# Linear attention and a SiLU MLP in one kernel: sums of x kept in one tile, two of them placed sooner, and two streams of pieces exchanged in the last half group

## The chip, the cores and the metric

The kernel runs on one core of a Trainium2 chip. The metric is device time in microseconds (us), the median of several runs. Engines are named as in the profile: PE is the matrix engine, PEld its weight loads, DVE the vector engine, ACT the scalar engine, POOL the GpSimd engine, SP the engine that here only issues DMAs.

## The reference

```python
# q, k, v, alpha: (4, 8, 768, 48), float32; w_in and w_out: float64
for t in range(S):
    state = alpha[:, :, t, :, None] * state + einsum('bhd,bhe->bhde', k[:, :, t], v[:, :, t])
    y[:, :, t] = einsum('bhd,bhde->bhe', q[:, :, t], state)
x = y.transpose(0, 2, 1, 3).reshape(3072, 384)
h = x @ w_in              # w_in  384 x 2048
g = h * (1 / (1 + exp(-h)))
out = g @ w_out           # w_out 2048 x 384
```

That is a decayed running state for each of 32 heads, and an MLP on what it gives; the output is 3072 rows of 384 numbers.

## The kernel before, in words

**Two halves at once.** The attention part walks over 24 blocks of 128 tokens (`NT = 24`), one block a step, four slots a step. The MLP part trails behind it: four blocks make a group of 512 tokens, six groups in all (grp 0 to 5, `GB = 4`, `NG = 6`). Its work is cut into generators that advance one piece at a time; `fill(step, slot)` runs pieces after each slot until the work done reaches what is due. Once the start is over (`late` is filled), every matmul is recorded in program order, so PE runs exactly the order in which pieces are called.

**The w_in side.** Groups 2 to 5 use a bilinear scheme with fewer products: `enter(grp, pair)` forms 20 block products (`PRODUCTS`) of sums of x and sums of w_in, for one of two halves ("pairs") of the columns. It has seven pieces; here they are E0 to E6. E0 to E5 have three products each and E6 two; one product is four PE instructions in the trace. Products go into three PSUM banks `ps_m`, are evicted by ACT (L936) or combined by DVE (L944, L587), pass SiLU on ACT (L941), and end with one addition for each half of the tokens, `side_by_side` (L1019). E6 holds the last two products; after them come, on DVE, the sums written `tt(s[0])` and `tt(s[3])`, on ACT the SiLU of each, and then the two `side_by_side`.

**The sums of x.** `sums_x(grp)` is one piece of no counted work: it takes a tile `xc` of 11 blocks of 128x256 from a pool with one buffer, and DVE forms 11 sums in a fixed order (`SUMS_X`, lines L582 to L587). The first two, blocks 9 and 6, need only the first half of a group's tokens; the third needs the second half. E0's products read sums 9, 6 and 6; E1's first product reads sum 15, which is the eighth of the list.

**The w_out side.** `leave(grp, h)` forms, for half a group, seven products with blocks of w_out; pieces L0 to L6, of eight matmuls, that is 16 PE instructions in the trace. They go to two PSUM banks `ps_o`. L6 fills the first bank and DVE adds to it into the output tile (`store`, L1042); L0 of the next `leave` fills that same bank again, from new. L0 reads first the g of pair 0, then (from its fifth matmul) that of pair 1.

**The order.** `pieces` is a list written out by hand. For group grp the list holds `sums_x(grp)`, and then by turns one piece of `leave(grp - 1, h)` and one of `enter(grp, pair)`: L0 E0 L1 E1 ... for pair 0 with h 0, and the same for pair 1 with h 1. After the last group, `leave(5, 0)` and `leave(5, 1)` follow alone. `pieces[done][2]` is the number of blocks whose x must exist; `phases` says where groups end in the list, and `marks` at which slot each is due.

**The audits.** `audit()` reads alpha, w_in and w_out once more, a piece a time, into one buffer (`late["look"]`, one buffer), and two DVE reductions a piece (L685) keep a largest and a smallest value. SP issues the next load (L677) when the second reduction of the one before has ended. The weights are 8-byte numbers, so one piece of w_out, 128x384, is 384 KB; of these there are 16. The reductions stand in DVE's order between the work of the pieces, in an order that is kept. From all of them DVE makes a flag that decides at the end whether the general path must run.

**DVE's order** is made by a scheduler except where `tc.keep_in_program_order` is called: the sums of x and the reductions keep their order among each other, all else is placed by it.

Of the kernel before, what the change touches and what calls it, by code (L numbers as in the profile page):

```python
# [8 lines left out]
F32 = mybir.dt.float32  # L9
# [10 lines left out]
def general(  # L20
# [322 lines left out]
SUMS_X = (  # L343
    (9, 1, 2, 1, 4), (6, 1, 0, 1, 2), (7, 1, 2, 1, 3), (8, 1, 0, 1, 7), (10, -1, 1, -1, 8),
    (11, 1, 5, -1, 10), (12, 1, 4, 1, 11), (15, -1, 0, 1, 12), (16, 1, 1, -1, 15),
    (13, 1, 4, 1, 7), (14, -1, 6, 1, 11),
)
# [8 lines left out]
def quotients(  # L356
# [22 lines left out]
    late = {}  # L379
# [25 lines left out]
    GB = 4  # L405
    NG = NT // GB
    HF = NFT // 2
    NQ = NFT // 4
    TB = GB * C // 2
    HO = HD // 2  # L410

    def pool(name, bufs=1, space=None):
        kw = {} if space is None else {"space": space}
        return ctx.enter_context(tc.tile_pool(name=name, bufs=bufs, **kw))
# [51 lines left out]
    def load(n, names="akq"):  # L466
        if n == NT:
            return
        c = ctxs.setdefault(n, dict(zip(("ci", "b"), divmod(n, B))))
        b, rows = c["b"], slice(c["ci"] * C, c["ci"] * C + C)  # L470
        for name, src in (("a", alpha), ("k", k), ("q", q)):
            if name not in names:
                continue
            x = src[b, :, rows, :]
            if n < NA:
                c[name] = nat[name][n % NIN]
                nc.sync.dma_start(c[name][:, :, 0:D], x.transpose([1, 0, 2]))
                continue

            c[name] = late["quads"][name]
            for u in range(2):
                for i in range(2):
                    r = 64 * u + 32 * i
                    nc.sync.dma_start(
                        c[name][r : r + 32, 32 * (1 - i) :][:, 0 : 4 * NP * D].rearrange(
                            "p (g c) -> p g c", g=NP),
                        x[u::2].rearrange("h (b j) d -> b h (j d)", j=4))
# [90 lines left out]
    def combine(to, sa, a, sb, b):  # L580
        if sa == sb == 1:
            return dve.tensor_tensor(to, a, b, ALU.add)  # L582
        if sa == 1:
            return dve.tensor_tensor(to, a, b, ALU.subtract)
        if sb == 1:
            return dve.tensor_tensor(to, b, a, ALU.subtract)  # L586
        return dve.scalar_tensor_tensor(to, a, -1.0, b, ALU.mult, ALU.subtract)  # L587
# [100 lines left out]
    xts, xcs = {}, {}  # L688
# [183 lines left out]
    def block_x(grp, at):  # L872

        if at < 2 * NKT:
            return xts[2 * grp + at % 2][:, at // 2, :]
        return xcs[grp][:, at - 2 * NKT, :]

    def sums_x(grp):
        xcs[grp] = late["xc"].tile([128, len(SUMS_X), TB], F32, name="xc")
        for to, sa, a, sb, b in SUMS_X:  # L880
            tc.keep_in_program_order(
                combine(block_x(grp, to), sa, block_x(grp, a), sb, block_x(grp, b)))
        yield
# [8 lines left out]
    turn = [0, 1, 2]  # L892
# [217 lines left out]
    def group(grp):  # L1110
        return [[(enter(grp, pair), 12, GB * grp + GB)] * 7 for pair in range(2)]

    def output(grp):
        return [[(leave(grp, h), 12, GB * grp + GB)] * 7 for h in range(2)]

    def both(x, y):
        for i in range(max(len(x), len(y))):
            pieces.extend(x[i : i + 1] + y[i : i + 1])

    pieces = []  # L1120
# [4 lines left out]
    phases = [len(pieces)]  # L1125
# [2 lines left out]
    phases.append(len(pieces))  # L1128
    before = output(1)
    for grp in range(2, NG):  # L1130
        pieces.append((sums_x(grp), 0, GB * grp + GB))
        for x, y in zip(before, group(grp)):
            both(x, y)
        phases.append(len(pieces))
        before = output(grp)
    pieces += before[0] + before[1]
# [17 lines left out]
    def settle():  # L1154

        first.close()
        late.update(look=pool("look"), part=pool("part"), xc=pool("xc"), turn=pool("turn"),
                    wx=pool("wx").tile([128, 8, NQ, 128], F32, name="wx"))
        quads = pool("quads")
        late["p"] = pool("p").tile([128, NP * W + 1], F32, name="p")  # L1160
        late["quads"] = {name: quads.tile([128, 32 + 4 * NP * D], F32, name=f"{name}t") for name in "akq"}
        for name, t in late["quads"].items():
            gps.memset(t, 1.0 if name == "a" else 0.0)
        load(NA)
# [20 lines left out]
    for step in range(STEPS):  # L1185
        if step == 1:
            load(NIN)
        stages = [[(scores, 1)], [(products, 0)], [(values, 1)], [(states, 1)]]
        if step == 1:

            stages = stages[1::-1] + stages[2:]
        elif step >= NA:
            stages = [[(land, 1), (scores, 1)], [(products, 0)], [(quotient, 0)],
                      [(values, 1), (states, 1), (flip, 0)]]
        for slot, group in enumerate(stages):
            for stage, lag in group:
                n = step - lag
                if not 0 <= n < NT:
                    continue
                stage(n)  # L1200
                if stage is values:
                    bridged = n + 1
                if stage is states and n + 1 + NIN < NA:
                    load(n + 1 + NIN)
                if stage is states and n + NV < NT:
                    load_v(n + NV)
            if step * SLOTS + slot == (NA + 1) * SLOTS - 1:
                x = decayed.rearrange("p (o i c) -> p o i c", o=2, c=C)
                for r, o in later:
                    gps.memset(x[r, o, :, 0:CH], 0.0)  # L1210
            fill(step, slot)
            if step * SLOTS + slot >= NA * SLOTS - 1 and conv_done[1] == NFT and not late:
                settle()
# [35 lines left out]
@with_exitstack  # L1249
def kernel(  # L1250
    ctx: ExitStack,
    tc: tile.TileContext,
    q: bass.AP,
    k: bass.AP,
    v: bass.AP,
    alpha: bass.AP,
    moe_w_in: bass.AP,
    moe_w_out: bass.AP,
    out: bass.AP,
):  # L1260


    flag = ctx.enter_context(tc.tile_pool(name="flag", bufs=1))
    small = flag.tile([1, 1], I32, name="small")
    args = (q, k, v, alpha, moe_w_in, moe_w_out, out)
    within = quotients(tc, small, *args)
    with tc.If(within < 1, label="general"):
        general(tc, *args)
# [30 lines left out]
```

## Time and profile before

| what | value |
|---|---|
| median of 3 runs | 559.94 us (559.90 to 559.98) |
| span of the profiled execution, first to last instruction | 558.1 us |
| what lies between that span and the median | 1.8 us |
| busy PE, PEld, DVE, ACT, POOL | 541.4, 488.8, 445.1, 208.4, 75.9 us |
| mean granted PE clock | 0.994 |
| reductions of the audits (L685) | 65, from 247.2 to 518.4 us |
| last block of attention leaves PE | about 443 us |
| pair 1 of group 5 begins on PE | about 479 us |

The page gives busy time by engine for one profiled execution. The list of waits names, for each engine, what ended its idle time. The timeline gives start, length, engine, line, operation and tiles, the number of instructions merged, and in brackets the idle time before it. A row's length is that of its instructions from the first start to the last end; neighbours on DVE and PE overlap, so the step from start to start is what an instruction costs in a full queue. Starts of PE instructions are 0.163 us apart for a 128x192 product and 0.216 us for a 128x256 one where nothing is waited for, which makes a piece L 2.61 us, E0 to E5 2.59 us and E6 1.73 us.

### The profile page before, as it was taken

To read this page: it belongs to the slowest core of one execution; us is meant where nothing else is said; L and a number is where in the kernel's file an instruction comes from. 1 tells how busy PE (TensorE), PEld (TensorE's weight loads), DVE (VectorE), ACT (ScalarE), POOL (GpSimd) and SP (SyncE) were. 2 spreads that over 40 slices of the span, in tenths; PEclk is the share of its full clock that TensorE was granted. 3 is DMA by queue.
4 is the path that set the end of the run, shared out by engine and by line. 5 is a ranking of instruction groups with operands and counts; after the bars stand their busy time and mean duration, and the time that the engine had idled before them with its cause. 6 is when DMAs were issued, how large, how long until landed. Compare 5 with 4: busy or idle time off the path is not lost. (4 is left out here: it accounts for less than half of the span.)

```text
span 558.1 us, 12640 instructions
## 1 busy us (share of the span) xinstructions
PE 541.4 (97%) x5026; PEld 488.8 (88%) x5026; DVE 445.1 (80%) x801; ACT 208.4 (37%) x466; POOL 75.9 (14%) x146
## 2 busy tenths in 40 slices
PE   5999999999999999999999999999999999999996
PEld 3788887998899898899999999988998999998996
DVE  5887889974999799997998986998894775857531
ACT  3456643223333243353353353353263341432200
POOL 4100010221211211021021021021121000001000
PEclk9799999999999999999999999999999999999999
DMA  9999861164445525355445654717712122333101
GB/s 218 255 276 177 232 189 40 38 164 108 126 131 136 142 62 134 88 145 157 129 109 142 194 141 115 198 22 179 180 48 84 53 99 95 111 109 106 38 25 32
DMA packets 99220, 70.13 MB, mean 126 GB/s; under 512 B 56272, under 2 KB 88656, under 8 KB 99152
## 3 DMA queue, kind: packets, MB, share of 16 engines
q1 hardware_dynamic: 97232, 65.30, 44.6%
q0 software_dynamic: 1920, 3.93, 2.0%
q8 instruction: 41, 0.67, 0.5%
q14 instruction: 27, 0.22, 0.1%
HBM read 61.34 MB, written 7.86 MB: 124 GB/s over the span
## 5 line engine op out<-in xcount | busy, mean ns | idle before, releaser
L388 PE MATMUL ps_o<-w_out,g 128*128 128x192 f32 x768 | 134.7, 329 | 1.1 <-DVE o L1042 0.9
L388 PEld LDWEIGHTS ps_o<-w_out,g 128*128 128x128 f32 x768 | 125.4, 190 | 5.1 <-DVE o L1042 2.3
L388 PE MATMUL ps_m<-xt,w_in 128*128 128x256 f32 x480 | 113.6, 383 | 1.5 <-ACT xt L851 1.1
L388 PEld LDWEIGHTS ps_m<-xt,w_in 128*128 128x128 f32 x480 | 89.1, 190 | 14.4 <-ACT xt L851 1.6
L388 PE MATMUL ps_o<-wt,g 128*128 128x192 f32 x576 | 99.7, 326 | 0.0
L388 PEld LDWEIGHTS ps_o<-wt,g 128*128 128x128 f32 x576 | 95.1, 190 | 1.6 <-issue 0.2
L388 PE MATMUL ps_m<-xc,w_in 128*128 128x256 f32 x288 | 70.7, 382 | 0.0
L685 DVE TENSOR_REDUCE seen<-bits 128x1 f32<-128x384 int32 (+2 forms) x65 | 42.5, 689 | 24.0 <-DMA bits<-in_moe_w_out_dram 19.6
L388 PEld LDWEIGHTS ps_m<-xc,w_in 128*128 128x128 f32 x288 | 53.6, 190 | 7.0 <-DVE g L944 0.3
L941 ACT ACTIVATE g<-g 128x1024 f32<-128x1024 f32 x32 | 33.0, 1056 | 59.0 <-DVE g L944 59.0
L1033 DVE TENSOR_TENSOR g<-g 128x512 f32<-128x512 f32 x72 | 49.8, 708 | 6.1 <-PE ps_o L388 6.1
L1045 POOL DMA_DIRECT2D out_dram<-o x40 | 22.0, 550 | 223.2 <-DVE o L1042 127.6
L813 POOL TENSOR_SCALAR_AFFINE_SELECT g<-g 64x256 f32<-64x256 f32 x64 | 34.2, 534 | 124.8 <-ACT g L806 105.8
L388 PE MATMUL ps_m<-xc,wx 128*128 128x256 f32 x192 | 50.0, 383 | 1.0 <-DVE xc L586 1.0
L936 ACT COPY g<-ps_m 128x512 f32<-128x512 f32 x64 | 36.5, 588 | 36.5 <-PE ps_m L388 36.4
L388 PEld LDWEIGHTS ps_m<-xc,wx 128*128 128x128 f32 x192 | 35.2, 190 | 5.3 <-ACT u L1064 1.3
L944 DVE TENSOR_TENSOR g<-ps_m,g 128x512 f32<-128x512 f32 x56 | 37.0, 684 | 2.9 <-PE ps_m L388 2.7
L722 DVE TENSOR_TENSOR_SCAN u<-al,one 128x516 f32<-128x516 f32 x24 | 30.0, 1249 | 10.6 <-ACT al L719 10.3
L909 ACT ACTIVATE g<-ps_m 128x512 f32<-128x512 f32 x32 | 19.1, 596 | 42.8 <-PE ps_m L388 42.3
L936 ACT COPY part<-ps_m 128x512 f32<-128x512 f32 x32 | 18.9, 589 | 43.0 <-DVE g L944 21.3
L752 DVE TENSOR_TENSOR_SCAN p<-al,inv 128x516 f32<-128x516 f32 x24 | 29.9, 1246 | 1.0 <-PE ps_a L388 0.4
L388 PE MATMUL ps_a<-g,vn 128*32 128x128 f32 x768 | 27.5, 278 | 1.8 <-POOL g L801 1.7
(126 smaller groups left out, 611.4 us busy)
## 6 DMA issues: line engine op xcount, KB each, us to landing
bits<-in_moe_w_in_dram SPq DMA_DIRECT2D x24, 512.0 KB, 4.8
bits<-in_moe_w_out_dram SPq DMA_DIRECT2D x32, 384.0 KB, 3.1
at<-in_alpha_dram SPq DMA_DIRECT2D x64, 96.0 KB, 2.5
kt<-in_k_dram SPq DMA_DIRECT2D x64, 96.0 KB, 2.5
qt<-in_q_dram SPq DMA_DIRECT2D x64, 96.0 KB, 2.6
bits<-in_alpha_dram SPq DMA_DIRECT2D x9, 512.0 KB, 3.8
out_dram<-o POOLq DMA_DIRECT2D x40, 96.0 KB, 2.4
flips<-turn SPq DMA_DIRECT2D x12, 256.0 KB, 2.4
```

The costliest lines, as they stand in the source:

```text
L388: in_order(nc.tensor.matmul(*args, **kw))
L685: dve.tensor_reduce(seen[kind][which][:, i : i + 1], x, axis=AX, op=op, apply_absolute_value=True))
L722: dve.tensor_tensor_scan(u[:, end - 1 :: -1], sg[:, end:0:-1], one[:, end:0:-1], 0.0, ALU.mult, ALU.add)
L752: dve.tensor_tensor_scan(p[:, 0:end], sg[:, 0:end], iv[:, 0:end], 0.0, ALU.mult, ALU.add)
L813: gps.affine_select(x, x, pattern=[[0, NP], [1, CH]], compare_op=ALU.is_ge, fill=0.0, base=0, channel_multiplier=-1)
L909: act.activation(gts[grp, h, pair][:, i : i + 2, q % 2, :], ps, AF.Silu)
L936: act.copy(to, ps)
L941: act.activation(x, x, AF.Silu)
L944: dve.tensor_tensor(to, a, b, op)
L1033: dve.tensor_tensor(cells(grp, h, pair, *to), cells(grp, h, pair, *x), cells(grp, h, pair, *y), ALU.subtract)
L1045: (gps if grp < NG - 1 else nc.sync).dma_start(out[r : r + C, c * HO : (c + 1) * HO], o)
```

## The change

The tile of sums is made once and kept (`late["xc"]` is now the tile and not a pool). `sums_x` stops after its first two sums and goes on at a second call; the first call is put into the list two pieces ahead of the end of the group before, with a demand of two blocks of the group and not four. For pair 1 of group 5 alone, the two streams are exchanged: E0 L0 E1 L1 ... E6 L6.

```diff
     def sums_x(grp):
-        xcs[grp] = late["xc"].tile([128, len(SUMS_X), TB], F32, name="xc")
-        for to, sa, a, sb, b in SUMS_X:
+        xcs[grp] = late["xc"]
+        for i, (to, sa, a, sb, b) in enumerate(SUMS_X):
+            if i == 2:
+                yield
             tc.keep_in_program_order(
                 combine(block_x(grp, to), sa, block_x(grp, a), sb, block_x(grp, b)))
         yield
...
     for grp in range(2, NG):
-        pieces.append((sums_x(grp), 0, GB * grp + GB))
-        for x, y in zip(before, group(grp)):
-            both(x, y)
+        sums = sums_x(grp)
+        pieces.insert(len(pieces) - 2, (sums, 0, GB * grp + 2))
+        phases[-1] += 1
+        pieces.append((sums, 0, GB * grp + GB))
+        for pair, (x, y) in enumerate(zip(before, group(grp))):
+            both(*((y, x) if grp == NG - 1 and pair == 1 else (x, y)))
         phases.append(len(pieces))
         before = output(grp)
...
-        late.update(look=pool("look"), part=pool("part"), xc=pool("xc"), turn=pool("turn"),
+        late.update(look=pool("look"), part=pool("part"), turn=pool("turn"),
+                    xc=pool("xc").tile([128, len(SUMS_X), TB], F32, name="xc"),
                     wx=pool("wx").tile([128, 8, NQ, 128], F32, name="wx"))
```

## The prediction, made before the changed kernel ran

> **What bounds the kernel now.** I read the page's busy times first, then the list of waits for PE, then the timeline around each wait.
>
> ```profile
> PE 541.4 (97%) x5026; PEld 488.8 (88%) x5026; DVE 445.1 (80%) x801; ACT 208.4 (37%) x466; POOL 75.9 (14%) x146
> ```
> PE is busy 97% of the span and the change takes no matmul away. Only PE's waits can be won or lost. In the list of waits those of the trailing part are few:
>
> ```profile
> PE ps_m L388 <- DVE g L944: 1.3, 2, 0.9
> ...
> PE ps_m L388 <- DVE xc L586: 1.0, 1, 1.0
> PE ps_o L388 <- DVE o L1042: 0.9, 2, 0.7
> ```
> All name DVE. The timeline has their places: one each in group 2, at the start of group 4, and at the end of group 5.
>
> ```profile
> 188.43 0.69 DVE L1019 TENSOR_TENSOR g<-g 128x512 f32<-128x512 f32 x1 [2.49 <-ACT g L909]
> ...
> 218.62 0.69 DVE L944 TENSOR_TENSOR g<-ps_m,g 128x512 f32<-128x512 f32 x1
> 219.37 1.13 PE L388 MATMUL ps_m<-xt,wx 128*128 128x256 f32 x4 [0.92 <-DVE g L944]
> ...
> 362.40 1.10 DVE L582 TENSOR_TENSOR xc<-xt 128x256 f32<-128x256 f32 x3
> ...
> 369.22 0.40 DVE L586 TENSOR_TENSOR xc<-xc,xt 128x256 f32<-128x256 f32 x1
> 369.77 1.10 PE L388 MATMUL ps_m<-xc,wx 128*128 128x256 f32 x4 [1.02 <-DVE xc L586]
> ...
> 513.75 1.00 DVE L685 TENSOR_REDUCE seen<-bits 128x1 f32<-128x384 int32 x2
> 514.67 0.68 DVE L587 SCALAR_TENSOR_TENSOR g<-g 128x512 f32<-128x512 f32 x1
> 515.27 0.35 DVE L1042 TENSOR_TENSOR o<-ps_o,u 128x192 f32<-128x192 f32 x1
> 515.68 3.25 PE L388 MATMUL ps_o<-w_out,g 128*128 128x192 f32 x16 [0.71 <-DVE o L1042]
> ```
> The wait at 369.77 is not for the first two sums but for the eighth (block 15). At 515.68 PE waits for the output addition that frees L0's bank; it stood behind two reductions. How full DVE is beside these places decides what moved work costs there; in windows (busy time, then instructions):
>
> ```profile
> 188.40:219.00 30.60, 30.08 (x59) 1.00 0.36 95
> 347.10:369.70 22.60, 22.54 (x42) 1.00 0.53 138
> 477.30:519.00 41.70, 28.57 (x57) 1.00 0.33 107
> ```
> Full from 188.4 to 219 and from 347.1 to 369.7, and with gaps after 477.3. Those gaps belong to the reductions, which wait for their loads:
>
> ```profile
> 505.72 1.01 DVE L685 TENSOR_REDUCE seen<-bits 128x1 f32<-128x384 int32 x2 [2.46 <-DMA bits<-in_moe_w_out_dram]
> 509.64 1.01 DVE L685 TENSOR_REDUCE seen<-bits 128x1 f32<-128x384 int32 x2 [0.91 <-DMA bits<-in_moe_w_out_dram]
> ```
> One pair about every 4.0 us: 1.0 of reductions, then 3.0 until the next load has landed. This chain runs at its own pace.
>
> [...]the operation at 218.62 reads a product that was finished on PE before 213, and stood behind a scan of 1.49 us. [...]the loads of L677 have a median of 3.2, and about 3.0 in the last half. [...]Here three sums of 0.42 us take 1.10 together: 0.34 a step, the price I use.
>
> **The change part by part.** No instruction and no DMA is added; on every engine the counts stay. By the order of the changed program POOL's and SP's queues are untouched, PE's and ACT's orders differ only in pair 1 of group 5, and DVE's at the four group starts and there. The kept tile is priced at nothing: its sums wait for no PE read in the new order, since the readers of blocks 9 and 6 are two pieces back. A gain from it alone is excluded, as no wait for the tile's release is in the trace.
>
> *Group 2: -0.64.* The two sums now stand ahead of the transposes at 182.9, so they fall into DVE's 2.49 us of idle time before 188.43. From there to 218.62 DVE has no idle time to lose, and does 0.64 less (190.39 to 191.02, two steps). PE was ready at 217.42 + 4 x 0.216 = 218.28 and waited 1.08; 0.44 remain. What comes later on DVE and PE moves with it. Bounds: 0 to -1.08.
>
> *Group 3: 0.* PE waits for nothing there before. The sums go ahead of L587 at 271.80, and the g that L0 needs is finished over a microsecond before its fifth matmul.
>
> *Group 4: 0.* This is the stall that the edit seems to aim at. But DVE is full from 347.1 on, and the sums are put in at 354.6, inside that stretch. All between moves 2 x 0.34 = 0.68 later, the queue behind is 0.68 shorter, and sum 15 ends where it did, at 369.62. Queued behind the two sums are the output addition at 358.03 (0.36 long, needed by L0 at 359.66: 0.6 of room) and the last additions of E6, whose SiLU then ends at 360.76; L0's fifth matmul is due at 359.66 + 8 x 0.163 = 360.96. If that waits a little, the later stall shrinks by as much. Bounds: -0.68 to +0.2.
>
> *Group 5, start: 0.* No PE wait before; DVE has 0.5 of idle time that takes the sums. The reductions standing among the sums come 0.16 earlier, and with them the chain of loads.
>
> *Group 5, exchange: +0.99.* In the clock of before:
> - E0 directly follows E6 of pair 0 (PE ends it at 477.27 + 1.73 = 479.00). The wait of 0.23 that L0 had at 479.24 goes. E0's second product fills the bank that DVE frees at 479.78; PE gets there at 479.00 + 0.86 = 479.86. I take 0; at most 1.0, if a pair of reductions gets between; a gain is excluded.
> - Pieces of 2.6 us follow: E6 begins at 510.2, and waits 0.1 for an addition behind the reductions of 509.5. L6 follows and ends at 514.64.
> - In the new order of DVE the next-to-last pair of reductions stands *ahead* of E6's two additions (L944), and L6's output addition behind the first `side_by_side`. The load for that pair landed just before 513.75; 0.16 earlier gives 513.39. Two steps of 0.46: first addition 514.31 to 514.99; its SiLU on ACT, 1.06 long, 515.04 to 516.10; `side_by_side` from 516.13, a step of 0.60; output addition 516.73 to 517.09; L0 on PE at 517.15.
> - Before, L0 began at 515.68 and took until 518.77, since it also waited inside for SiLU (3.09 in place of 2.61). Now it is free inside: 517.15 + 2.61 = 519.76. So +0.99.
>
> The last two `leave` and the end are the same on all engines after that. Sum: -0.64 + 0.99 = **+0.35 us**. Against the profiled span of 558.1 that is 558.45; the median lies 1.8 above that span, so 559.94 + 0.35 = 560.3. About 0.2% (1.1 us) is what a measurement of this kernel can tell from no change.
>
> **The rivals.**
> 1. *The reductions do not bind (faster).* If loads land sooner, L6's addition follows L6 at once. What such a turn costs is seen at the end of the next `leave`: L6 ends at 534.70, L0 begins at 535.36, so 0.66 (of which one early matmul of L1 fills a half). Then L0 begins at 515.3 and ends at 517.9, 0.86 better than before; with group 2, -1.5: 558.4. For it: loads of this size took between 2.7 and 3.5 here. Against it: most reductions in this stretch wait for their load, and L944 now stands behind one.
> 2. *The chain of loads comes later (slower).* L0 of `leave(5, 0)` now starts 3.7 us after the load before the last one has landed, and each microsecond that this is late is one of the run. From 449.35 on, 16 loads follow each other; at 0.08 more each, 1.3: 561.6. It decides for slower from 0.8 on. For it: no other work can make up for it, as PE has nothing else in its order. Against it: the mean of the 16 was steady.
> 3. *Group 2 gains nothing* because what moves there (the state additions L868, transposes) keeps DVE waiting elsewhere: +1.0: 560.9. Against it: 30.08 of 30.60 us busy.
> 4. *The change does what it seems to aim at:* the wait for the sums at 369.77 goes, -1.0 more: 559.3. Against it: DVE's full window.
>
> **How the numbers follow.** Forecast with its small variations 0.55, rival 1 0.12, rival 2 0.20, rivals 3 and 4 0.13, both within 0.2%. Faster is rival 1 (part of it): 0.12; slower is rival 2 and a little of 3: 0.22; within: 0.66. Range 558.9 to 561.6: it holds the forecast, the nearer half of rival 1 and rival 2 up to its price.
>
> **What would show it.** In the profile after: PE's wait in group 2 near 219 down to about 0.4; the wait for L586 at the start of group 4 still about 1.0; no wait where pair 1 of group 5 begins; and a single PE wait of 2 to 2.5 us for `o` L1042 before `leave(5, 0)`, with two reductions ahead of L944 on DVE. Wrong if that wait is under 1 us, if the L586 wait is gone, or if PE stalls inside pair 1.

## The result, and the profile after

The changed kernel takes 563.73 us (median of 6 runs, 561.31 to 564.70), beside 560.06 us (559.90 to 560.47, 6 runs) for the kernel before on the same chip. The ratio is 1.0052, 95% interval 1.0037 to 1.0067: slower by about half a per cent, 3.7 us. The profiled execution of after has a span of 562.9 us and a time of 564.68 us, at the upper end of its runs; before's span was 558.1.

The list of waits for PE, of the kernel after (engine, operation, what released it: us in total, times, longest):

```profile
PE ps_m L388 <- DVE g L946: 3.1, 4, 1.7
PE ps_o L388 <- DVE o L1044: 2.9, 3, 2.4
...
PE ps_m L388 <- DVE xc L586: 1.0, 1, 1.0
```
The wait for L586 at the start of group 4 is what it was. The waits for the additions of g (L946, which was L944) have grown from 1.3 to 3.1 us, those for `o` (L1044, was L1042) from 0.9 to 2.9. The timeline of PE gives their places:

```profile
217.60 1.03 PE L388 MATMUL ps_m<-xt,wx 128*128 128x256 f32 x4
...
367.74 1.10 PE L388 MATMUL ps_m<-xc,wx 128*128 128x256 f32 x4 [0.98 <-DVE xc L586]
...
479.58 1.13 PE L388 MATMUL ps_m<-xc,w_in 128*128 128x256 f32 x4 [0.69 <-DVE g L946]
...
512.71 1.13 PE L388 MATMUL ps_m<-xt,w_in 128*128 128x256 f32 x4 [1.72 <-DVE g L946]
...
518.89 4.55 PE L388 MATMUL ps_o<-w_out,g 128*128 128x192 f32 x16 [2.45 <-DVE o L1044]
```
The first row stood at 219.37 before with a wait of 0.92 us in brackets; now there is none. The three last rows are new: E0 behind E6, the second product of E6, and L0 of `leave(5, 0)`. The last of them is also long: 16 instructions took 4.55 us, where 16 such take 2.76 elsewhere (2.87 after a wait). DVE's timeline before those two waits:

```profile
511.04 1.01 DVE L685 TENSOR_REDUCE seen<-bits 128x1 f32<-128x384 int32 x2 [2.20 <-DMA bits<-in_moe_w_out_dram]
511.97 1.28 DVE L946 TENSOR_TENSOR g<-ps_m,g 128x512 f32<-128x512 f32 x2
...
515.14 1.01 DVE L685 TENSOR_REDUCE seen<-bits 128x1 f32<-128x384 int32 x2 [0.63 <-DMA bits<-in_moe_w_out_dram]
516.07 1.28 DVE L946 TENSOR_TENSOR g<-ps_m,g 128x512 f32<-128x512 f32 x2
517.87 0.69 DVE L1021 TENSOR_TENSOR g<-g 128x512 f32<-128x512 f32 x1 [0.52 <-ACT g L943]
518.48 0.35 DVE L1044 TENSOR_TENSOR o<-ps_o,u 128x192 f32<-128x192 f32 x1
```
Twice DVE stands idle until a load has landed, reduces it, and only then adds what PE is waiting for. The load behind the row at 511.04 was issued at 506.68 and landed at 511.02, 4.34 us later; its neighbours took between 2.9 and 3.2. The order on DVE is the forecast one: two reductions ahead of L946, `side_by_side` (L1021) ahead of `o`.

The long L0 is explained by a window (busy PE, instructions, granted clock, DMA share, GB/s):

```profile
518.90:522.50 3.60, 3.60 (x12) 0.53 0.08 27
```
TensorE's granted clock fell to half for about 3.4 us (0.53 over 3.60 us is half for 94% of it): 12 instructions in 3.60 us, starts 0.320 us apart in place of 0.163.

**Where the 4.8 us between the two spans lie**, from one PE instruction to the same one in the other trace (always the first one after the last attention product of a step):

| stretch, time before | before | after | difference |
|---|---|---|---|
| start to 193.3 | 193.3 | 192.6 | -0.7 |
| groups 2 and 3, to 363.3 | 170.0 | 168.7 | -1.3 |
| group 4, to 426.9 | 63.6 | 64.4 | +0.8 |
| from there to the last PE instruction | 126.6 | 132.3 | +5.6 |
| after it | 4.6 | 4.9 | +0.3 |

The differences are of unrounded values. The first row varies by 2 us from one execution to another (192.0 to 194.1 over the kernels below, whose work is the same until there). The fourth is the exchange, in start-to-start excess: E0 0.85 less the old 0.23, so +0.6; E6 +1.9; L0 2.61 less the old 0.87 and the 0.28 inside it, so +1.5; half clock +1.7 (ten steps of 0.320 in place of 0.163, and a little in the steps on both sides). Unrounded they make 5.6.

### The profile page after: what moved, and what is told of

It reads as the page before. It is cut to its first block, busy times and chain, and to the rows that moved or that the text cites. A ratio compares the mean times of both kernels' runs of the same rounds, so it can differ in the third digit from the quotient of the medians.

```text
span 562.9 us, 12636 instructions
## 1 busy us (share of the span) xinstructions
PE 543.9 (97%) x5026; PEld 491.0 (87%) x5026; DVE 445.8 (79%) x801; ACT 208.5 (37%) x466; POOL 76.9 (14%) x146
## 5 line engine op out<-in xcount | busy, mean ns | idle before, releaser
L388 PEld LDWEIGHTS ps_o<-w_out,g 128*128 128x128 f32 x768 | 127.2, 192 | 6.1 <-DVE o L1044 3.7
L943 ACT ACTIVATE g<-g 128x1024 f32<-128x1024 f32 x32 | 33.1, 1055 | 64.0 <-DVE g L946 63.9
L946 DVE TENSOR_TENSOR g<-ps_m,g 128x512 f32<-128x512 f32 x56 | 36.9, 680 | 2.3 <-PE ps_m L388 2.0
```

The source lines that it names most:

```text
L388: in_order(nc.tensor.matmul(*args, **kw))
L943: act.activation(x, x, AF.Silu)
L946: dve.tensor_tensor(to, a, b, op)
```

## The experiments

The theory at the outset (A): the sums gain, and the exchange loses all, because it puts work that PE waits for behind reductions that wait for loads. Rivals: the sums bring the loss by bringing PE sooner to whatever the loads pace (B), or the new order costs by itself, whatever the loads do (C). A ratio is always to the kernel before, run on the same chip.

### Each part alone

`x1_sums_only` is after without the exchange, `x6_kept_only` has the kept tile alone, and `x2_exchange_only` the exchange alone:

```diff
# x1: after, but
-            both(*((y, x) if grp == NG - 1 and pair == 1 else (x, y)))
+            both(x, y)
# x2: before, but
-        for x, y in zip(before, group(grp)):
-            both(x, y)
+        for pair, (x, y) in enumerate(zip(before, group(grp))):
+            both(*((y, x) if grp == NG - 1 and pair == 1 else (x, y)))
# x6: before, but
-        xcs[grp] = late["xc"].tile([128, len(SUMS_X), TB], F32, name="xc")
+        xcs[grp] = late["xc"]
...                                   # and the tile is made once, as in the change
```

> Only the first half of the change: sums of x in a kept tile, the first two of a group made two pieces sooner; the exchange in the last half is left out. Theory A (the exchange puts additions and o behind reductions that wait for loads, and lets TensorE's clock fall; the sums only gain): the waits near 513 and 519 us are gone, the half clock too, and about half of the 1.2 us gained at group 2 is kept: 559.0 to 559.8 us. Rival B (the early sums bring the loss, by bringing TensorE sooner to everything that is paced by loads): 562 to 564 us, with waits of over 1 us in the last half.

> Only the second half of the change: the exchange of the pieces in the last half; sums and their tile as before. Theory A: waits of 1 to 3 us for the additions of E6 near 513 us and for o near 519 us, and a half clock after them: 563.0 to 564.5 us. Rival B (the sums bring the loss): 560 to 561 us.

> Only the tile of the sums is kept for the whole run; the sums stand where they stood, the pieces too. All theories that blame order or loads: 559.8 to 560.3 us, no change. Rival: the place of the tile or its dependencies cost: over 561 us.

| kernel | median us | ratio | interval | groups 2, 3 | group 4 | rest |
|---|---|---|---|---|---|---|
| x1, sums | 559.72 | 0.9982 | 0.9972 to 0.9993 | 169.0 | 63.6 | 127.5 |
| x2, exchange | 563.75 | 1.0057 | 1.0035 to 1.0079 | 170.0 | 63.9 | 131.5 |
| x6, kept tile | 560.58 | 0.9999 | 0.9982 to 1.0015 | 169.6 | 63.6 | 128.5 |

The last three columns are stretches of the table above. The loss comes whole from the exchange; the sums are a small gain, and the kept tile is nothing. B is out. In x2 the half clock is there as well: PE idle 2.31 us before L0, then a clock of 0.5. The rest of 126.6 to 128.5 us for three kernels of the same order of pieces (before, x1, x6) shows how much that stretch moves from run to run; with the three buffers below it is 125.3 to 125.4 us for the same order, which points to the loads.

### Loads that come early

The w_out loads of the audits go by turns into three buffers: the one they had, and two tiles that the attention part has done with by then. The next load no longer has to wait for the reductions of the last. Everything else stays.

```diff
-            t = late["look"].tile([128, 512, 2], I32, name="bits")
+            if n == HD and at[1] % 3:
+                t = late["quads"]["ak"[at[1] % 3 - 1]][:, 32:].bitcast(I32).rearrange("p (n w) -> p n w", w=2)
+            else:
+                t = late["look"].tile([128, 512, 2], I32, name="bits")
```
This was put into all four combinations of the change's halves: neither (`x4_before_look3`), the sums (`x7_sums_look3`, and again `x12_sums_look3_again`), the exchange (`x8_exchange_look3`), both (`x3_after_look3`).

> The changed kernel, but the loads for the reductions of w_out go in turn to three buffers instead of one, so that a load is issued up to two reductions sooner and no reduction waits long for it. Theory A: the reductions end in time, the waits near 513 and 519 us fall below 0.5 us each, the clock stays at 1.0, and the time is 558.5 to 559.8 us. Rival C (the order of the pieces itself costs, by the banks that E0 after E6 takes at once, or by the work of VectorE in sum, whatever the loads do): 562 to 564 us, and the waits stay.

> The kernel before with the same three buffers. It says what the buffers alone are worth. Theory A (before, a load is in time for TensorE but for some tenths): 559.0 to 560.0 us. Rival C: 560 us, nothing.

> Early sums and kept tile, no exchange, and three buffers for the loads of the reductions of w_out. Theory A: the gain of group 2 (1.2 us) is kept whole since no reduction waits long: 558.2 to 559.2 us. Rival: the gain is given back at another wait: 559.5 to 560.3 us.

> The exchange and the three buffers, sums as before. Theory A: the exchange costs nothing once the loads are early: within 0.5 us of the kernel before with three buffers, 559.2 to 560.2 us. Rival C (the order of the pieces costs by itself): 562 us or more.

> Early sums and kept tile with three buffers, without the exchange, once more, beside the three others on their chip: 556.8 to 557.3 us.

| kernel, three buffers | median us | ratio | interval | groups 2, 3 | group 4 | rest |
|---|---|---|---|---|---|---|
| x4, neither | 558.16 | 0.9963 | 0.9949 to 0.9977 | 169.7 | 63.7 | 125.3 |
| x7, sums | 556.88 | 0.9928 | 0.9912 to 0.9945 | 168.7 | 63.8 | 125.3 |
| x12, sums again | 556.86 | 0.9921 | 0.9897 to 0.9946 | 168.7 | 64.1 | 125.4 |
| x8, exchange | 559.19 | 0.9970 | 0.9957 to 0.9982 | 169.9 | 63.9 | 126.6 |
| x3, both | 558.13 | 0.9960 | 0.9943 to 0.9977 | 168.7 | 63.5 | 126.6 |

With early loads the changed kernel gets 0.9960 where it had 1.0052, while the kernel before gets 0.9963. So about 5 us of the changed kernel's time hung on loads through one buffer, and some 2 us of the old one's. That is more than was expected: x3, x4 and x7 are faster than their ranges, while x8 is not within 0.5 us of x4 by its median. The two waits at E0 and E6 are gone from x3, and its clock stays at 1.00 from 505 to 530. C is out as the main cause, but a part of it is true: the traces still show the exchange 1.3 us behind (126.6 beside 125.3, twice; by the ratios 0.4 and 1.8, each uncertain by about 1), at one place. DVE and PE of x3:

```profile
511.79 0.69 DVE L1024 TENSOR_TENSOR g<-g 128x512 f32<-128x512 f32 x1 [0.26 <-ACT g L946]
512.74 0.69 DVE L1024 TENSOR_TENSOR g<-g 128x512 f32<-128x512 f32 x1 [0.25 <-ACT g L946]
513.35 1.00 DVE L688 TENSOR_REDUCE seen<-bits 128x1 f32<-128x384 int32 x2
...
514.36 0.35 DVE L1047 TENSOR_TENSOR o<-ps_o,u 128x192 f32<-128x192 f32 x1
```

```profile
514.76 2.87 PE L388 MATMUL ps_o<-w_out,g 128*128 128x192 f32 x16 [1.36 <-DVE o L1047]
```
No load is waited for any more; `o` is late because two `side_by_side`, which wait for SiLU, and two reductions stand in front of it.

### The place of o

`x11_both_late_side` is x3 with the last two `side_by_side` emitted later, at the start of the `leave` that needs them. `x15_o_first` also holds the order of `o` and them.

```diff
# x11: x3, but
         for h in range(2):
-            side_by_side(grp, h, pair)
+            if (grp, pair) != (NG - 1, 1):
+                side_by_side(grp, h, pair)
...
     # in leave(grp, h), ahead of L0
+        if grp == NG - 1:
+            side_by_side(grp, h, 1)
# x15: x11, and o of L6 in leave(4, 1) and those two side_by_side go through in_order(...)
```

> Changed kernel with three buffers, and the two side_by_side of pair 1 of group 5 are emitted at the start of leave(5,0) and of leave(5,1) instead of in E6, so that they stand behind the output addition o on VectorE. If the 1.3 us that the exchange still costs with early loads is the place of o behind them (and SiLU, for which they wait): L0 of leave(5,0) waits under 0.4 us, and 556.8 to 557.3 us. Rival: o waits for something else (the reductions ahead of it, the end of L6), and 557.8 to 558.4 us.

> Changed kernel with three buffers, side_by_side of pair 1 of group 5 at the start of leave(5,0) and leave(5,1), and the order of o before them held. If the place of o behind side_by_side is what the exchange still costs: L0 of leave(5,0) waits under 0.6 us, the time 557.0 to 557.6 us. Rival: the wait stays at 0.9 to 1.4 us, 557.8 to 558.4 us.

x11 took 557.77 us (0.9940, 0.9917 to 0.9963), and L0 still waited 0.87: the scheduler had put both `side_by_side` ahead of `o` again, so x11 tests nothing of what it was built for. In x15 they stand behind it (DVE, then PE):

```profile
513.25 0.36 DVE L1050 TENSOR_TENSOR o<-ps_o,u 128x192 f32<-128x192 f32 x1 [0.39 <-PE ps_o L388]
513.52 0.68 DVE L1025 TENSOR_TENSOR g<-g 128x512 f32<-128x512 f32 x1
```

```profile
513.66 2.87 PE L388 MATMUL ps_o<-w_out,g 128*128 128x192 f32 x16 [0.45 <-DVE o L1050]
```
`o` now waits only for the end of L6 on PE (0.39 us), though the last two reductions still stand ahead of it, at 511.26. x15 took 557.25 us (0.9939, 0.9923 to 0.9956); its rest is 125.7, so by the traces 0.9 of the 1.3 us have come back. By the times it is not shown, as the interval overlaps that of x3. The remaining 0.4 is about the wait of 0.45, for the turn from L6 straight to L0 through one bank.

### The half clock

`x5_after_warm` is after with two products of no use (identity by a row of ones, 128x512, into a free bank) at the start of `leave(5, 0)`, where PE would be idle. The output doesn't see them.

```diff
+        if grp == NG - 1 and h == 0:
+            warm = ps_attn(512)[:, 0, :]
+            for i in range(2):
+                pe.matmul(warm, lhsT=ident, rhs=one[:, 0:512], start=True, stop=True)
```

> The changed kernel with two added products of the identity with a row of ones (128x512 each, estimated at 1.7 us together from the pitch of the kernel's other fp32 products) ahead of L0 of leave(5,0), into a bank that nobody reads: they fill the idle time of TensorE before 519 us and add nothing to the output. If the half clock after 519 us follows from TensorE's idle time before it and costs 1.8 us by itself: clock 1.0 there, wait for o as before, and 561.5 to 562.5 us. Rival: the half clock has another cause, or its 1.8 us would be waited for anyway: 563 to 564.5 us.

```profile
514.15 1.88 PE L388 MATMUL ps_a<-one,ident 128*128 128x512 f32 x4
516.49 2.87 PE L388 MATMUL ps_o<-w_out,g 128*128 128x192 f32 x16 [0.46 <-DVE o L1044]
```
L0 takes 2.87 us and not 4.55, and the clock is 1.00. The time is 561.55 us, ratio 1.0015 (1.0005 to 1.0025) beside 1.0052 without the fillers: about 2 us less for work added. In this trace the waits at E0 and E6 were also shorter by about 1 us together, so the traces alone would give more; by the medians the clock's share is near the 1.7 counted above, with an uncertainty of about 1.

Then the other way: an idle time made on purpose in x3, which has none of over 1.4 us there. `x9_hold2` and `x10_hold4` put two and four products on VectorE ahead of `o`:

> Changed kernel with three buffers, and two added products of 128x512 on VectorE (ones and zeros of a constant with themselves, its values stay; 0.6 us each) just ahead of the output addition o that L0 of leave(5,0) waits for. PE's one idle time there grows from 1.4 to about 2.6 us, with no other wait before it. Theory D (an idle time of about 2.5 us halves TensorE's clock for 3.4 us): 1.2 + 1.8 = 3.0 us more than with three buffers alone, about 561.1 us, PEclk 0.5 after it. Rival E (it takes the earlier wait at E6 too, or a longer one): 1.2 us more, about 559.3 us, PEclk 1.0.

> The same with four added products: one idle time of about 3.8 us. Theory D: 2.4 + 1.8 = 4.2 us more than with three buffers alone, about 562.3 us. Rival E in its form that two waits are needed: 2.4 us more, about 560.5 us, PEclk 1.0.

Both failed as experiments. The added products depend on nothing, so the scheduler had them run at 406 to 413 us (the rows of `one`, L1049), the wait of L0 stayed at 1.36 us, and the times were 558.54 and 558.88 us. `x13_hold_o4` and `x14_hold_o9` write the same `o` from the same bank four and nine times before its sum, which can't be moved:

```diff
+                if (grp, h, m, c) == (NG - 2, 1, 1, 0):
+                    for _ in range(4):            # 9 in x14
+                        dve.tensor_tensor(o, x, y, ALU.subtract)
                 dve.tensor_tensor(o, x, y, ALU.add)
```

> Changed kernel with three buffers; o of L6 before leave(5,0) is written four times over (the differences, of no use) before its sum, each 128x192 from the same bank, about 0.3 us each, so that L0 waits 2.4 to 2.8 us instead of 1.4, with no other wait near. Theory D (an idle time of about 2.5 us by itself halves the clock): PEclk 0.5 after it, 1.2 + 1.8 = 3.0 us more than with three buffers alone (558.1): about 561.1 us. Rival E (it takes a longer one, or the wait at E6 as well): PEclk 1.0, about 559.3 us.

> The same with nine: L0 waits 3.6 to 4.2 us. [...]2.5 + 1.8 = 4.3 us more than with three buffers alone, about 562.4 us, PEclk 0.5. If a single idle time of that length does not: about 560.6 us.

x13 took 561.36 us (1.0012, 1.0001 to 1.0024), x14 564.76 us (1.0071, 1.0054 to 1.0088). From x13, L0 and a window after it:

```profile
516.03 4.55 PE L388 MATMUL ps_o<-w_out,g 128*128 128x192 f32 x16 [2.95 <-DVE o L1050]
```

```profile
516.40:519.70 3.30, 3.30 (x12) 0.50 0.09 30
```
In this trace one idle time of 2.95 us, with no other near it, is followed by the half clock; 1.36 us in x3 was not. So theory D holds for it, and rival E does not: neither a longer wait nor a second one is needed. The stretch behind 426.9 is 3.3 us longer than in x3, 1.6 of it the longer wait and 1.7 the clock. In x14 PE was idle for 4.90 us, more than aimed at (so 564.76 us and not 562.4), the clock was at half for 6.8 us from 517.31 on, and nearly the whole L0 ran at it (16 instructions in 5.26 us).

But the length of the wait does not decide alone. In before a wait of 1.66 us for `g` (L801, POOL) ends at 13.83, and the clock is at half from 15.40 to 22.23. In x1 the wait for the same line is as long, 1.7 us, and the clock stays full (mean of the execution 1.000). In after the wait of 1.72 us at E6 was not followed by a fall either: the clock is 1.00 from 505 to 518.90. Nor was the 1.36 us of x9 and x10 (1.00 from 505 to 526). Before, then x1 (busy PE, instructions, granted clock; the other two columns are of DMA):

```profile
11.99:15.40 3.41, 1.65 (x51) 1.00 1.08 383
15.40:22.23 6.83, 6.83 (x72) 0.50 1.21 269
```

```profile
10.04:13.45 3.41, 2.33 (x25) 1.00 1.08 381
13.45:16.87 3.42, 2.72 (x76) 1.00 1.16 318
16.87:24.00 7.13, 6.26 (x93) 1.00 1.23 250
```
Nor does the clock fall in every execution. A half clock of 3.41 us lowers the mean clock of an execution by 0.003. Of the six of x2, two have a mean clock of 1.000 and took 562.0 and 562.5 us; the four with 0.995 or 0.996 took 563.7 to 565.2. In x13 four of 20 have 0.998, which leaves no room for it, and took 559.3 to 560.3 us, near the 559.3 that rival E expected; the others took 560.7 to 563.2. Of the changed kernel's six, only the fastest (561.31 us, 0.998) leaves no room for it. How long PE waited in these executions is not shown, as none of them is a profiled one.

## Why the prediction was wrong, by its own steps

The prediction gave 560.3 us with a range to 561.6 and most of the chance to "no change"; the kernel came out at 563.7. Its direction was that of rival 2. Of its own signs, the L586 wait of about 1.0 and the wait of 2 to 2.5 us for `o` came true; the sign of being wrong, that PE stalls inside pair 1, came true as well, at E6. Step by step:

- **Group 2, -0.64: right in kind, too small.** The wait at 219.37 is gone whole, since DVE's operation that ends it came 1.9 us sooner (216.69 for 218.62, of which 0.7 is the earlier start), and the scan ahead of it took 1.23 us and not 1.49. The stretch of groups 2 and 3 is 1.0 to 1.3 us shorter with the sums in each pair of traces that differs by them and the tile (before and x1, x2 and after, x4 and x7, x8 and x3). The price of 0.34 a step holds, and what overlaps is 0.08 us of a row of 0.42 (and 0.09 of one of 0.69).
- **Group 3 and the start of group 4, 0: right.** The L586 wait stands at 0.98 us. Rival 4 is out.
- **Group 4 later: not counted.** In after, PE came earlier and met a w_in reduction that waited 2.03 us for its load, at 396.05; 0.8 us went back. It is not so in every trace: x1 and x3 lose nothing there, x7 0.2, x12 0.6.
- **"I take 0; at most 1.0, if a pair of reductions gets between" (E0 behind E6): the upper bound came true**, 0.85 us: a pair of reductions stood at 477.04, ahead of the additions that free the bank.
- **"E6 [...] waits 0.1": the first step that failed.** It waited 1.9. Its second product starts 1.69 us after the landing of the load whose reductions stand ahead of its addition (the same in x2 and x5), and that landing was dated by before's trace: the steps had the reductions at 509.5, after has them at 511.04. The load came 4.34 us after its issue, about 1.3 us later than its neighbours. With one buffer the chain of load, reductions, load took 62.9 us for 15 turns, 4.19 each, where before it took 4.04. The 13 turns ahead of the late load took 4.11 each, beside 4.05 before, so the price of rival 2, 0.08 a turn, fits them; the late load is what it lacked. But no load as late as that is needed: in x2 this load took 3.43 us, in x5 3.26, and E6 still waited 1.5. It was bad luck, too, that the dates came from the fastest of the six traces with one buffer (4.04 in before, 4.09 to 4.19 in x1, x5, x2, x6 and after).
- **L0 of `leave(5, 0)`: the mechanism right to 0.01 us, the date wrong.** The steps put L0 3.76 us after the landing of the next-to-last load. It came 3.77 us after it (515.12 to 518.89), in x2 and x5 the same. Only the landing was 1.7 us later than 513.39. Against loads that don't bind (x3, x8) the exchange costs 1.3 us, where the prediction had +0.99 with the loads of before.
- **2.61 us for L0 itself: the second step that failed.** It took 4.38 to the next piece (523.27), 0.1 of it the longer first step behind a wait (16 instructions took 2.87 there and 2.76 elsewhere). The prediction foresaw a wait of 2 to 2.5 us and took the work behind it at full clock: 1.7 us were missing from the sum, in this trace, though by the mean clocks not in every execution. Before's own trace has a fall of this kind at its start, 6.83 us at a clock of 0.50.
- **Rival 1, early loads let L0 start at once: half true.** The E6 wait goes, but L0 waits 1.36 us for `o`, whose place it had not counted; with `o` first (x15) the wait is 0.45, near the 0.66 it took from the end of the next `leave`.

The error in one sentence: the loads were taken at the dates they had in one trace, on a path where nothing can make up for a late one, and the wait so formed was long enough to slow, where the clock fell, what followed it.

What stays open: why the load issued at 506.68 took 4.34 us, why the half clock lasts 6.83 us in before and 6.8 in x14 but 3.41 in after, and what besides the length of a wait decides whether it comes (1.66 us in before, 1.72 at E6 in after).

## What to carry to other kernels

Before work that the bound engine waits for is moved behind work paced by loads, price that order with loads a microsecond late, not with the dates of one trace: here the same exchange cost 1.3 us by the traces (0.4 to 1.8 by the medians) with loads in time, and 3.2 to 3.9 by the medians with loads through one buffer. A check or a reduction of no hurry wants its own buffers: two more of them took 2 us off the kernel before, and with the early sums they make the version with the lowest median here, 556.9 us (0.9928; the interval of x15 overlaps it). And price a wait on TensorE of the length met here, 2.3 to 3.0 us, twice: once as idle time and once more, as a chance of 1.7 us, for the clock after it.

## What the hardware showed beyond that

Idle times of TensorE of 2.31, 2.45 and 2.95 us were followed by about 3.4 us at half clock in the traces of x2, after and x13, and one of 4.90 us in x14 went with 6.8 us of it, which began while PE was still idle; idle times of 1.36 us in x3, x9 and x10 were followed by none. A wait of 1.66 us at the start of before was followed by 6.83 us at half clock, one of 1.7 us in x1 and one of 1.72 us at E6 in after were not. Two products of no use, 1.88 us long, made the changed kernel about 2 us faster. Work until 193 us that is the same in all these kernels took between 192.0 and 194.1 us.
